# Re-ordering the opening loads, and four pair sums, of a linear-attention and token-mixer kernel

## Chip, core and metric

The kernel runs on one core of a Trainium2 chip. The metric is device microseconds of one execution. The text goes by two kinds of number: median times of several runs, and places in the trace of a single profiled run, where the start of one instruction is known to some hundredths of a microsecond. "Lead" below means how much earlier the same instruction starts in one trace than in the trace of the kernel before.

## The reference

```python
x = A_x                                        # 1 x 2048 x 1024, bf16
h = x + A(layernorm(x), wqkv, wo)              # linear attention, 32 heads
h2 = h + B(layernorm(h), w1, b1, w2, b2)       # MLP over the token axis, 3584 wide, gelu

def A(x, wqkv, wo):
    q, k, v = split(x @ wqkv)                  # heads of 32
    phi = lambda t: where(t > 0, t + 1, exp(t)) + 1e-6
    kv = einsum("bhsd,bhse->bhde", phi(k), v)
    z = einsum("bhsd->bhd", phi(k))
    o = (phi(q) @ kv) / (phi(q) @ z + 1e-6)
    return o @ wo
```

Only the very start matters here: tokens come in tiles of 128 rows. A tile is loaded, normalised (VectorE, ScalarE), transposed (TensorE), and multiplied by the key weights. Tiles 0 to 3 are done one by one with a plain product. From then on the kernel works on pairs of tiles ("runs") with a seven-product scheme, which needs sums and differences of blocks of the tokens ("pair sums") and of the weights ("weight sums").

## The kernel before: the parts concerned

The opening loads (`P` is 128, `CW` 512, `D` 1024, `ND` 8, `hk` 4). A contraction piece is 128 of the 1024 rows of the weights; "pieces 0-1" is `wkv[:, 0:2, 0:CW]`.

```python
def load_x(i, halves=False):
    x_sb = xload.tile([P, D], BF16, name="x_sb")
    if halves:
        nc.sync.dma_start(x_sb[:, 0:CW], x[i * P:(i + 1) * P, 0:CW])
        pin(nc.scalar.dma_start(x_sb[:, CW:D], x[i * P:(i + 1) * P, CW:D]))
    else:
        nc.sync.dma_start(x_sb[:], x[i * P:(i + 1) * P, :])
    return x_sb
# ...
xs = {0: load_x(0, True)}
xs[1] = load_x(1)
for k in (0, hk // 2):                                     # pieces 0-1, 2-3: ACT queue
    pin(nc.scalar.dma_start(wkv[:, k:k + hk // 2, 0:CW], wqkv_v[:, k:k + hk // 2, D:D + CW]))
nc.sync.dma_start(wkv[:, hk:ND, 0:CW], wqkv_v[:, hk:ND, D:D + CW])   # pieces 4-7
# ...
xs[2] = load_x(2)
for k0 in (0, hk):                                         # the other 512 key columns, two halves
    nc.sync.dma_start(wkv[:, k0:k0 + hk, CW:D], wqkv_v[:, k0:k0 + hk, D + CW:2 * D])
for i in range(3, G0 + 2):
    xs[i] = load_x(i)
```

The first products, in program order (every operation is pinned in its place on its engine):

```python
pin(ln[1][1](0))                 # VectorE: statistics of tile 1's first half
norm_halves(0)                   # VectorE: tile 0 normalised
transpose_first(0, 0, 0)
# ...
k_parts(0, 0, range(0, 6))       # tile 0, first key columns, pieces 0 to 5
norm_halves(1)
transpose_first(1, 6, ND)        # tile 1 transposed, pieces 6 and 7 of tile 0 between
ln_stats(2)
stats(2)                         # ScalarE: tile 2's scale
k_unit(1, 0)
# ...
k_unit(0, 1)                     # tile 0, other key columns
# ...
transpose_in(2)                  # TensorE transposes, ScalarE copies
ln_stats(3)                      # VectorE
stats(3)                         # ScalarE, behind the copies of tile 2
# ...
w_sums(kmov, slice(0, 1))
norm_halves(3)
# ...
k_unit(1, 1)
transpose_in(3)
```

And the pair sums in front of run 1, whose first use is the product `p6`:

```python
w_sums(vmov, slice(2, 4))
proj_unit(1, NDC + 1, pin)
ln_finish(G0 + 1)
x_sums(1)
# ...
v1.p1()
q_fill()
kv_accum(0)
kv_accum(1)
v1.p6()
```

## Time and profile before

| | before |
|---|---|
| time, median of the first 3 runs | 559.61 us (559.16 to 560.11) |
| profiled span | 558.6 us |
| TensorE busy | 551.3 us, 99% |
| VectorE, ScalarE busy | 444.0, 288.7 us |
| granted TensorE clock | 0.999 |

The page puts TensorE first everywhere, so the reading is about TensorE's few idle pieces; the prediction shows the view of waits and the timeline of TensorE for them. One view that the prediction did not use belongs here, because it turns out to hold the answer: the chain of work that ended last, in order of time. Its columns are start, duration, and what the chain was on; this is the kernel before.

```profile
4.08 9.13 DMA x_sb<-in_A_x_dram
...
13.23 1.30 DVE st L855 x2
...
15.36 1.22 DVE shared_sb L938
16.58 0.34 DVE xn L865
...
16.96 0.72 PE tp L1176 x8
```

The chain runs from the issue of tile 3's load straight to its landing at 13.21, through VectorE's statistics of that tile, a weight sum of 1.22 us (`w_sums(kmov, slice(0, 1))`) that stands in VectorE's order in front of the tile's normalisation, and the normalisation itself, to tile 3's transposes at 16.96. The longest wait of TensorE, the 1.56 us for weight pieces that the prediction names first, is not on it.

### The profile page before, as it was taken

How to read it: one execution, taken by the hardware profiler on the slowest of the kernel's cores; microseconds unless marked ns; L12 is line 12 of the kernel's file. 1: busy time of each engine (PE TensorE's matmuls, PEld its weight loads, DVE VectorE, ACT ScalarE, POOL GpSimd, SP SyncE). 2: the span in 40 equal slices, each digit the busy share in tenths (PEclk: the TensorE clock that was granted, in tenths of full speed). 3: DMA queues.
4: the chain of work that ended last, by engine and by line, in shares of the span. 5: the costliest groups of instructions: out<-in, count | busy, mean ns of one | idle time of the engine just before them, and what ended most of it. 6: DMA issues, size and time to landing. Idle time of an engine off the chain costs nothing.

```text
span 558.6 us, 8933 instructions
## 1 busy us (share of the span) xinstructions
PE 551.3 (99%) x3387; PEld 320.3 (57%) x3387; DVE 444.0 (79%) x858; ACT 288.7 (52%) x614; POOL 26.3 (5%) x36
## 2 busy tenths in 40 slices
PE   7999999999999999999999999999999999999997
PEld 3444446645444444456666766666444667767665
DVE  6898888764479688889989889897996978749747
ACT  4747778676777777645455565464310312413311
POOL 1000000000000000000000000000002103103111
PEclk9999999999999999999999999999999999999999
DMA  8933332201955961102240431414768759849434
GB/s 296 308 76 76 76 76 39 39 0 48 338 144 167 340 207 75 76 0 70 84 151 0 151 115 38 150 33 100 191 214 226 196 126 247 213 131 239 95 105 75
DMA packets 83931, 74.51 MB, mean 133 GB/s; under 512 B 15650, under 2 KB 76336, under 8 KB 83888
## 3 DMA queue, kind: packets, MB, share of 16 engines
q1 hardware_dynamic: 79104, 69.61, 41.7%
q0 software_dynamic: 4096, 3.68, 4.8%
q10 hardware_dynamic: 688, 0.66, 0.4%
q8 instruction: 26, 0.43, 0.3%
q14 instruction: 17, 0.14, 0.1%
HBM read 59.12 MB, written 11.67 MB: 127 GB/s over the span
## 4 chain that ended last, share of the span: by engine, by line
PE 90%; DMA 5%; DVE 3%; ACT 1%; issue 1%; SPq 0%; DVEq 0%; ACTq 0%
PE psI L234 23%; PE psC L234 14%; PE acc_t L234 14%; PE psB L234 8%; PE psB L964 4%; PE psC L964 4%; PE psA L964 4%; PE psA L346 2%; PE acc_t L1295 2%; PE psB L346 2%; DMA x_sb<-in_A_x_dram 2%; PE psE L964 2%; PE psC L346 2%; DMA wq<-in_B_w_dram 2%; PE acc_t L886 2%; PE psA L234 1%
## 5 line engine op out<-in xcount | busy, mean ns | idle before, releaser
L234 PEld LDWEIGHTS <-is 128*128 128x128 f16 x736 | 71.8, 98 | 31.2 <-DVE hi L234 0.4
L234 PEld LDWEIGHTS <-sa 128*128 128x128 f16 x606 | 59.2, 98 | 27.4 <-issue 0.2
L234 PEld LDWEIGHTS <-wq 128*128 128x128 bf16 (+1 forms) x496 | 48.4, 98 | 28.2 <-issue 1.0
L234 PE MATMUL acc_t<-wo_sb,pqT 128*128 128x512 f16 x256 | 55.6, 379 | 0.0
L491 POOL DMA_DIRECT2D out_dram<-wq x28 | 24.4, 935 | 520.6 <-ACT wq L494 489.1
L234 PEld LDWEIGHTS <-pqT 128*128 128x128 bf16 x256 | 24.9, 98 | 30.5 <-issue 0.6
L234 DVE TENSOR_TENSOR t<-psI,t 128x256 f32<-128x256 f32 (+1 forms) x45 | 20.8, 476 | 22.2 <-PE psI L234 20.9
L194 DVE TENSOR_SCALAR e_sb<-e_sb 128x512 bf16<-128x512 bf16 x64 | 18.5, 288 | 22.0 <-ACT e_sb L189 21.9
L234 PE MATMUL psC<-gs,wq 128*128 128x512 f16 x140 | 34.1, 379 | 0.0
L964 PEld LDWEIGHTS <-xs 128*128 128x128 f16 x208 | 20.0, 98 | 22.5 <-DVE xs L953 1.1
L234 PE MATMUL psC<-hT,sa 128*128 128x512 f16 x112 | 31.2, 379 | 0.0
L234 PE MATMUL psI<-hi,is 128*128 128x256 f16 x200 | 30.0, 273 | 0.0
L234 PE MATMUL psB<-hT,sa 128*128 128x512 f16 x112 | 29.7, 379 | 0.0
L234 PE MATMUL acc_t<-xnT,wq_sb 128*128 128x512 bf16 x128 | 29.5, 380 | 0.1
L189 ACT ACTIVATE e_sb<-acc_t 128x512 bf16<-128x512 f32 x32 | 19.1, 598 | 18.6 <-PE acc_t L1295 10.0
L234 DVE BATCH_NORM_STATS2 hst<-acc_t 128x6 f32<-128x512 f32 x32 | 21.4, 692 | 9.0 <-ACT h_bf L234 8.9
L964 PE MATMUL psA<-wkv,xnT 128*128 128x512 bf16 x104 | 26.7, 379 | 0.0
L964 PEld LDWEIGHTS <-xnT 128*128 128x128 bf16 x156 | 15.2, 98 | 18.1 <-issue 0.2
L234 PE MATMUL psC<-hT,wq 128*128 128x512 f16 x96 | 24.6, 379 | 0.0
L234 ACT CAST h_bf<-acc_t 128x512 bf16<-128x512 f32 x32 | 18.4, 581 | 12.0 <-PE acc_t L234 12.0
L234 DVE TENSOR_TENSOR e<-psI,es 128x256 f32<-128x256 f32 x20 | 8.5, 425 | 19.9 <-PE psI L234 17.8
L234 ACT COPY psI<-psI 128x256 f32<-128x256 f32 x50 | 18.0, 360 | 11.6 <-PE psI L234 9.7
(246 smaller groups left out, 1132.6 us busy)
## 6 DMA issues: line engine op xcount, KB each, us to landing
wq<-in_B_w_dram SPq DMA_DIRECT2D x14, 1024.0 KB, 7.9
wq<-in_B_w_dram SPq DMA_DIRECT2D x12, 896.0 KB, 8.0
gs<-parked SPq DMA_DIRECT2D x9, 896.0 KB, 4.8
shared_sb<-rd_dram SPq DMA_DIRECT2D x32, 128.0 KB, 3.8
out_dram<-h_bf SPq DMA_DIRECT2D x16, 256.0 KB, 2.0
x_sb<-in_A_x_dram SPq DMA_DIRECT2D x15, 256.0 KB, 3.0
w2o<-in_B_w_dram SPq DMA_DIRECT2D x4, 896.0 KB, 10.8
out_dram<-wq POOLq DMA_DIRECT2D x28, 128.0 KB, 5.0
```

What stands on the lines that cost most here:

```text
L189: pin(nc.scalar.activation(e_sb[:], src, ACT.Exp))
L194: pin(nc.vector.tensor_scalar(e_sb[:], e_sb[:], 1.0, PHI_EPS, ALU.min, ALU.add))
L234: return (lambda *a, **kw: pin(op(*a, **kw))) if self.always or getattr(Held, self.key) else op
L346: pe.matmul(ps[:, cols], lhsT=lhs[:, k, :], rhs=mv(k)[:, cols], start=(start and k == 0), stop=(k == self.nk - 1), skip_group_check=True,)
L491: nc.gpsimd.dma_start(to, ot[:, a:b], accum_op=ALU.add)
L886: mm = nc.tensor.matmul(pp[:, 0:CW], lhsT=xnT[:, kt, i * P:(i + 1) * P], rhs=wkv[:, kt, c * CW:(c + 1) * CW], start=(kt == 0), stop=(kt == ...
L964: pin(nc.tensor.matmul(ps[:], lhsT=lhs[:, k, :], rhs=rhs[:, k, :], start=(start and k == 0), stop=(k == hk2 - 1), skip_group_check=True,))
L1295: nc.tensor.matmul(qp[:, 0:SW], lhsT=wq_sb[:, kt, j * P:(j + 1) * P], rhs=xnT[:, kt, u * SW:(u + 1) * SW], start=(kt == 0), stop=(kt == ND ...
```

## The change

Intent: put the opening loads on SyncE in the order in which they are first wanted, so that pieces 2-3 no longer land behind pieces 4-7; let tile 1 come on the ACT queue beside them; fetch tile 3 in front of the second half of the other key columns; and make run 1's pair sums ahead of two weight sums that are wanted later.

```diff
-            def load_x(i, halves=False):
+            def load_x(i, halves=False, q=nc.sync):
 ...
-                    nc.sync.dma_start(x_sb[:], x[i * P:(i + 1) * P, :])
+                    dma = q.dma_start(x_sb[:], x[i * P:(i + 1) * P, :])
+                    if q is not nc.sync:
+                        pin(dma)
 ...
-            xs[1] = load_x(1)
-            for k in (0, hk // 2):
-                pin(nc.scalar.dma_start(wkv[:, k:k + hk // 2, 0:CW], wqkv_v[:, k:k + hk // 2, D:D + CW]))
-            nc.sync.dma_start(wkv[:, hk:ND, 0:CW], wqkv_v[:, hk:ND, D:D + CW])
+            xs[1] = load_x(1, q=nc.scalar)
+            for k0, k1 in ((0, hk // 2), (hk // 2, hk), (hk, ND)):
+                nc.sync.dma_start(wkv[:, k0:k1, 0:CW], wqkv_v[:, k0:k1, D:D + CW])
 ...
             for k0 in (0, hk):
                 nc.sync.dma_start(wkv[:, k0:k0 + hk, CW:D], wqkv_v[:, k0:k0 + hk, D + CW:2 * D])
-            for i in range(3, G0 + 2):
+                if k0 == 0:
+                    xs[3] = load_x(3)
+            for i in range(4, G0 + 2):
                 xs[i] = load_x(i)
 ...
+            x_sums(1)
             w_sums(vmov, slice(2, 4))
             proj_unit(1, NDC + 1, pin)
             ln_finish(G0 + 1)
-            x_sums(1)
```

## The prediction

> **What bounds the kernel now.** I read the page first. TensorE is busy for 551.3 of 558.6 us and leads the chain of work that ended last with 90%, at full granted clock in all 40 slices. So time can only be won where TensorE is idle, 7.3 us in all. The view of waits, filtered to TensorE and with no window, names every idle piece of it that a semaphore ended:
>
> ```profile
> PE acc_t L886 <- DMA wkv<-in_A_wqkv_dram: 1.6, 1, 1.6
> PE acc_t L98 <- DVE warm L88: 1.2, 1, 1.2
> PE tp L1176 <- DVE xn L865: 0.6, 2, 0.3
> PE psB L964 <- DVE xs L953: 0.3, 1, 0.3
> PE acc_t L234 <- ACT r_sb L191: 0.2, 1, 0.2
> ```
>
> Columns: total us, times, longest. All but the last row lie in the first 36 us. The 1.2 is the wait for the very first operand. So the whole stock that this change can reach is 1.6 + 0.6 + 0.3 = 2.5 us, 0.45% of the span. The rest of the idle time stands at the launch and behind the last matmul, and the change does not touch it.
>
> The timeline of TensorE places these pieces (start, duration, what, and in brackets the idle time before it):
>
> ```profile
> 6.08 0.72 PE L1176 MATMUL tp<-ident,xn 128*128 128x128 bf16 x8 [0.22 <-DVE xn L865]
> 6.94 0.60 PE L886 MATMUL acc_t<-wkv,xnT 128*128 128x512 bf16 x2
> 9.10 1.02 PE L886 MATMUL acc_t<-wkv,xnT 128*128 128x512 bf16 x4 [1.56 <-DMA wkv<-in_A_wqkv_dram]
> ...
> 16.96 0.72 PE L1176 MATMUL tp<-ident,xn 128*128 128x128 bf16 x8 [0.33 <-DVE xn L865]
> ...
> 35.56 1.04 PE L964 MATMUL psB<-wo_sb,xs 128*128 128x512 f16 x4 [0.28 <-DVE xs L953]
> ```
>
> The first projection runs its contraction pieces 0 and 1 at 6.94, then stands until 9.10, because pieces 2 and 3 of the key weights have not landed. At 16.96 it waits for token tile 3's normalised rows; at 35.56 for the pair sums of run 1. From 17.5 to 35.3 and after 36.4 TensorE never stands.
>
> The DMA view, windowed to single issues, gives the landings. Key-weight pieces 0-1 (ACT queue, issued 1.18) land at 5.0, tile 1 (SyncE, 1.20) at 4.4, pieces 4-7 (SyncE, 1.66) at 8.8, pieces 2-3 (ACT, 1.67) at 9.06, tile 2 (2.13) at 9.5; the two halves of the other key columns at 11.0 and 12.5, tile 3 at 13.2. The two loads that matter:
>
> ```profile
> wkv<-in_A_wqkv_dram SPq DMA_DIRECT2D x1, 512.0 KB, 7.2
> wkv<-in_A_wqkv_dram ACTq DMA_DIRECT2D x1, 256.0 KB, 7.4
> ```
>
> The last number is us to landing: a load half the size takes longer on the ACT queue. Pieces that are needed first come last.
>
> **What the Trainium skill says.** "DMA: Bandwidth & Descriptors", section "Queues, rings and completion order": each of the 16 engines takes turns between the queues that it has work for. The trace agrees: both loads above were issued within 0.01 us and end 0.2 us apart, so pieces 2-3 were held back by pieces 4-7. Same page, "Issuing engines are not separate DMA queues": another issuing engine brings no bandwidth, only issue time. So tile 1 on the ACT queue is a matter of order alone. Same page, "Specifications": about 358 GB/s from HBM for a core. The trace's stretches show 351 from 6 to 8 us, 373, 369, then 354 and 353: up to 4% above the page, and full from 6 us until 25 us. Nothing makes these loads faster; they can only be sorted. "VectorE: DVE Perf Modes", section "Side-by-side: where the cycles go for N=2048 bf16": about 1224 ns for a two-source 16-bit operation of that length; the trace has 1219 to 1226 ns for the weight sums.
>
> **The change part by part.** No arithmetic and no byte is added.
>
> *Key weights.* In order of need, 128 KB + 256 KB of tile 0's halves and pieces 0-1 come first on SyncE, beside 128 + 256 KB on ACT; then pieces 2-3 (1.05 MB in all by then), pieces 4-7 (1.57 MB), tile 2 (1.84 MB), the same sums as before for the last two. How fast these land is the uncertain size. The sixteen completion steps of each load stand in the trace. Until 5.2 us those of one load lie within 0.4 us of each other; for pieces 4-7 they spread from 6.2 to 8.84 with a middle of 7.1, so a few of the 16 engines fell behind by up to 1.8 us between 5 and 9 us. They never catch up before 24 us: the last step stays 1.4 us or more behind the middle one. Two cases follow.
>
> Case L (the lag returns): the slowest engine's landings by bytes are 0.79 MB at 5.0, 1.57 at 9.0, 1.84 at 9.5, 2.36 at 11.0. Then pieces 2-3 land at 5.0 + (1.05-0.79)/(1.57-0.79) x 4.0 = 6.3, pieces 4-7 at about 8.9. TensorE does pieces 0 to 3 from 6.94 to 7.8 (0.216 us each) and waits for piece 4 until 8.9, where it stood at 9.53 before: 0.6 us ahead. Tile 2 still lands at 9.5. The second half of the other key columns, now behind tile 3, comes at 3.15 MB, 13.2, where TensorE would want it at about 12.8: a new wait of 0.4 us, after which 0.2 us of lead are left. Tile 3 now lands at 11.8 instead of 13.2. That alone does not give 1.4: VectorE is at tile 2's normalisation until 12.4 (before, 12.82), so tile 3's statistics start 0.8 us earlier. ScalarE must copy tile 2's transposes, 0.2 us earlier, before it makes tile 3's scale; so the scale is at 16.0 instead of 16.22, the normalised rows start at 16.06 instead of 16.50, and the transposes of 16.96 start at 16.5. **Gain 0.4 us.**
>
> Case N (no lag): pieces 2-3 at 5.8, 4-7 at 7.4, tile 2 at 8.1, tile 3 at 10.3, the late key columns at 11.8. Pieces 0 to 5 run from 6.94 to 8.3, tile 1's transposes then wait for its rows (8.11, first half written 8.52), so TensorE is there at 8.55 instead of 9.96, 1.4 us ahead. The statistics of tiles 2 and 3 follow at once, and the transposes of 16.96 start at 15.5. **Gain 1.45 us.** The limit is then ScalarE and VectorE, no longer a load.
>
> *Tile 1 on ACT.* It trades places with pieces 0-1 and should land between 4.3 and 5.0. VectorE takes its first statistics at 4.93, so at worst this costs 0.1 us in front of tile 0's rows.
>
> *Pair sums earlier.* Four operations of 0.42 us, 0.35 to 0.45 from start to start, 1.47 together, move ahead of two weight sums (31.94 to 34.25). The second pair sum is then ready at about 33, where TensorE wants it at 35.28: the whole wait of **0.28 us** goes. In exchange, tile 5's normalisation goes from 34.16 to 35.6 and its transposing load lands at about 39.2 instead of 37.8. Its first reader is the pair sums of run 2 at 40.68, so 1.4 us remain. The third value-weight sum is ready at 34.6 and wanted at 39.9. VectorE's work is the same and it has 0.68 us of idle time at 39.85, so the 0.28 isn't given back.
>
> *Sum.* Case L: 0.4 + 0.28 = 0.7 us. Case N: 1.45 + 0.28 = 1.7 us. After 36 us TensorE has no wait but one of 0.2, so what is won there should reach the end one for one. I weigh L somewhat more than N, since the small bias loads and the traffic mix that lie in the same microseconds stay: 1.1 us. Before: 559.61. Predicted: **558.5 us**.
>
> **Rivals.** (1) *A wait takes the place of the one removed.* The late key columns behind tile 3, or tile 1's transposes, or tile 3's rows. Speaking for it: the load stream is full from 6 to 25 us, and landings in front of TensorE have under 1 us of slack. If it takes all, only 0.28 stays: 559.3. (2) *Tile 1 late on the ACT queue.* Its statistics stand in VectorE's fixed order ahead of tile 0's normalisation, so every 0.1 us beyond 4.93 delays the first transposes. Against it: the ACT queue's first 384 KB landed by 5.0 before. If it came at 6.0 as the ACT load of 7.4 us suggests, about 1 us would be lost at the start, though the weights would meanwhile arrive: 559.0 to 560.0. (3) *Nothing comes through,* because a later load or buffer sets the pace. Against it: TensorE has no idle time between 36 us and its end but 0.2. It would give 559.6. (4) All 2.5 us are gained, 557.1. Against it: tile 3's rows depend on ScalarE's and VectorE's chain.
>
> **Range and chances.** Case L to case N is 558.9 to 557.9; runs of the kernel before differ by 0.95 us (559.16 to 560.11), a median of three by some 0.4. I take 557.4 to 559.6. Two per cent would be 11.2 us, over four times the whole stock of 2.5 us, so faster has 1%. Slower would need a stall of 11 us that nothing here could make: 1%.
>
> **What would show it.** Right: the 1.56 us wait at 9.10 is gone or below 0.9, pieces 2-3 land before 7 us, the wait for pair sums at 35.56 is gone, TensorE starts its last transposes between 15.5 and 16.6. Wrong, if tile 0's transposes start later than 6.2 (rival 2), if the wait for the key columns of k_unit(0, 1) is over 0.5 us (rival 1), if tile 5's transposing load delays the sums of run 2, or if the lead at 36 us isn't found at the end of the span (rival 3).

## The result, and the profile after

| | before | after |
|---|---|---|
| time, median of 6 runs | 559.57 us (559.16 to 560.11) | 558.97 us (558.64 to 559.96) |
| ratio, 95% interval | 1 | 0.9992 (0.9979 to 1.0005) |
| second measurement: median, ratio | 559.60 us, 7 runs | 558.72 us, 4 runs; 0.9980 (0.9965 to 0.9995) |
| profiled span | 558.6 us | 557.7 us |

A ratio is the mean time of one kernel's runs over that of the other's in the same rounds, so it is not quite the ratio of the two medians. The second measurement excludes equality, the first does not; both point to half a microsecond or one.

First the view of TensorE's waits of the changed kernel, to be set against the five rows in the prediction (total us, times, longest):

```profile
PE acc_t L98 <- DVE warm L88: 1.2, 1, 1.2
PE acc_t L234 <- ACT r_sb L191: 0.4, 1, 0.4
PE tp L1179 <- DVE xn L867: 0.3, 1, 0.3
PE acc_t L888 <- DMA wkv<-in_A_wqkv_dram: 0.3, 1, 0.3
PE psB L234 <- ACT psB L530: 0.2, 1, 0.2
```

The 1.6 for key weights has become 0.3, and the row for pair sums is gone. In exchange a row that was 0.2 is 0.4 and a new one of 0.2 stands at the bottom; both lie far behind the opening. The timeline of TensorE in the changed kernel:

```profile
6.33 0.72 PE L1179 MATMUL tp<-ident,xn 128*128 128x128 bf16 x8 [0.33 <-DVE xn L867]
7.19 1.76 PE L888 MATMUL acc_t<-wkv,xnT 128*128 128x512 bf16 x6
...
12.72 1.02 PE L888 MATMUL acc_t<-wkv,xnT 128*128 128x512 bf16 x4 [0.26 <-DMA wkv<-in_A_wqkv_dram]
...
16.02 0.72 PE L1179 MATMUL tp<-ident,xn 128*128 128x128 bf16 x8
...
34.16 1.02 PE L966 MATMUL psB<-wo_sb,xs 128*128 128x512 f16 x4
```

Pieces 0 to 5 of tile 0 are now one row of six matmuls. The merged row hides a short wait: the fifth matmul starts 0.51 us behind the fourth (8.35 after 7.84, against a pace of 0.22), just behind the landing of pieces 4-7 at 8.31. The new wait at 12.72 is for the second half of the other key columns, which were put behind tile 3; the prediction foresaw it. Tile 3's transposes start 0.94 us earlier than before, run 1's product 1.40 us. The DMA view for single issues shows pieces 4-7 (512 KB) and pieces 2-3 (256 KB), with us to landing last:

```profile
wkv<-in_A_wqkv_dram SPq DMA_DIRECT2D x1, 512.0 KB, 6.1
wkv<-in_A_wqkv_dram SPq DMA_DIRECT2D x1, 256.0 KB, 4.3
```

The needed one comes first now. But the chain that ended last shows that the opening still hangs on a load, only on another one:

```profile
4.48 8.20 DMA wkv<-in_A_wqkv_dram
...
12.72 1.02 PE acc_t L888 x4
...
14.01 1.07 ACT xnT L1189 x2
15.08 0.20 ACT lnv L863
...
15.31 0.21 ACT rstd L864
...
15.54 0.42 DVE xn L867
...
16.02 0.72 PE tp L1179 x8
```

From the late key columns' landing at 12.68 the chain goes over the product that needs them, tile 2's transposes, ScalarE's copies of these, ScalarE's scale for tile 3, VectorE's normalisation, to tile 3's transposes.

A weight load is TensorE's instruction that takes in the fixed operand of the matmuls behind it; its rows are marked PEld. Following single weight loads through both traces (3400 in each; the same instructions in the same order) gives the lead: -0.25 us at tile 0's transposes, +1.48 at piece 2, +0.95 at tile 3's transposes, +1.45 at run 1's product, +1.25 at 156 us, +0.97 at the end. So half a microsecond of what was won at the opening was lost again later. Where and why is a question for the experiments.

### The profile page after: what moved, and what is told of

It is laid out like the page before. It is cut to its first block, busy times and chain, and to the rows that moved or that the text cites. A ratio compares the mean times of both kernels' runs of the same rounds, so it can differ in the third digit from the quotient of the medians.

```text
span 557.7 us, 8915 instructions
## 1 busy us (share of the span) xinstructions
PE 550.7 (99%) x3370; PEld 320.4 (57%) x3387; DVE 443.8 (80%) x858; ACT 288.8 (52%) x614; POOL 26.2 (5%) x36
## 4 chain that ended last, share of the span: by engine, by line
PE 91%; DMA 4%; DVE 2%; ACT 1%; SPq 1%; issue 0%; DVEq 0%; ACTq 0%
PE psI L234 23%; PE psC L234 14%; PE acc_t L234 14%; PE psB L234 8%; PE psC L966 4%; PE psB L966 4%; PE psA L966 4%; PE acc_t L888 3%; PE acc_t L1298 2%; PE psB L346 2%; PE psA L346 2%; PE psE L966 2%; PE psC L346 2%; DMA wq<-in_B_w_dram 2%; DMA wkv<-in_A_wqkv_dram 1%; PE kvps L917 1%
```

## The experiments

Twelve runs were made, of eight new kernels and four repeats, all with correct output. Two theories are compared. **Theory 1**, the prediction's: the wait for pieces 2-3 was what held TensorE, and the order of need removed it. **Theory 2**, from the chain: only the last of the loads that tile 3's transposes depend on counts, and the waits in front of it are interchangeable. Of the first four runs, the expectation of "tile 1 on SyncE" still rests on theory 1; theory 2 was written down, as the last landing plus a constant, after these four, from their traces. Then a further question came up: is the landing of that last load a matter of chance or of layout?

### Each part alone

Sums alone:

```diff
 # the kernel before, with only
+            x_sums(1)
             w_sums(vmov, slice(2, 4))
             proj_unit(1, NDC + 1, pin)
             ln_finish(G0 + 1)
-            x_sums(1)
```

> The kernel before with the pair sums moved and its loads untouched. Theory: nothing moves ahead of 31 us, so the transposes of tile 3 start at 16.96 as before (within 0.2), and run 1's product with the second pair sum starts 0.46 us earlier than before (35.1 instead of 35.56), since TensorE's weight loads stood 0.46 us there although the waits view shows 0.28. Rival: only the 0.28 us shown as idle comes back (35.28). Time: 0.3 to 0.5 us less than before, within the noise of the runs.

Measured: 559.17 us (median of 4), ratio 0.9990 (0.9974 to 1.0005). Transposes of tile 3 at 16.86, run 1's product at 34.95 (weight load) instead of 35.55: the lead grows from 0.10 to 0.60, so the pair sums are worth **0.50 us**, not 0.28. The reason is visible in the weight-load row of the kernel before:

```profile
35.55 0.55 PEld L964 LDWEIGHTS <-xs 128*128 128x128 f16 x4 [0.46 <-DVE xs L953]
```

The matmul row has 0.28 us of idle time in front of it, this one 0.46. Ends of matmuls are modelled and overlap the next ones, so the idle time in front of a matmul is too small a number for what a wait costs; start to start the trace has 0.56 against a pace of 0.06 here.

This run holds something more valuable. Its loads are those of the kernel before, yet pieces 2-3 landed at 7.10 instead of 9.06, and the waits read:

```profile
PE tp L1176 <- DVE xn L865: 1.5, 2, 1.0
PE acc_t L98 <- DVE warm L88: 1.2, 1, 1.2
PE acc_t L886 <- DMA wkv<-in_A_wqkv_dram: 0.5, 1, 0.5
```

The wait for weights fell from 1.6 to 0.5 without any change to it, and all that came of it at tile 3's transposes is 0.10 us: the wait for tile 3's rows grew to 1.0. Theory 1 is in doubt from here on.

Loads alone:

```diff
 # the changed kernel, with
-            x_sums(1)
             w_sums(vmov, slice(2, 4))
             proj_unit(1, NDC + 1, pin)
             ln_finish(G0 + 1)
+            x_sums(1)
```

> The changed kernel with the pair sums put back behind the weight sums. Theory: the loads alone give the 0.95 us lead at tile 3's last transposes (16.0 against 16.96), and the wait for the pair sums comes back, so the lead at run 1's product is 0.95 and not 1.45. Rival: with TensorE earlier the wait for the pair sums grows beyond 0.46 and the lead falls under 0.8. Time: some 0.5 to 0.9 us below before.

Measured: 559.04 us (4 runs), ratio 0.9987 (0.9971 to 1.0004). Lead 1.30 at tile 3's transposes, more than the changed kernel's 0.95 with the same loads, because the late key columns landed at 12.34 instead of 12.68. No growth up to run 1's product: the wait for pair sums is back in full (start-to-start 0.55). It did not grow with the lead either, so the rival fell. The two parts add up: the sums give 0.50 us with the old loads (0.10 to 0.60) and with the new ones (0.95 to 1.45).

### Which load counts

Tile 3 back behind both halves of the late key columns:

```diff
             for k0 in (0, hk):
                 nc.sync.dma_start(wkv[:, k0:k0 + hk, CW:D], ...)
-                if k0 == 0:
-                    xs[3] = load_x(3)
+            xs[3] = load_x(3)
```

> The changed kernel with tile 3 back behind both halves of the other key columns. Theory: the new 0.26 us wait at 12.7 is gone, but tile 3 lands 1.5 us later (12.7), its normalised rows start near 16.1 instead of 15.5 and the transposes near 16.5, so about 0.4 us of the 0.95 are lost (lead 0.4 to 0.6). Rival: tile 3's place does not matter because ScalarE's chain sets its rows; then the lead is 1.2.

Measured: 559.83 us (4 runs), ratio 1.0000 (0.9985 to 1.0015). Tile 3 landed at 12.75, the transposes started at 16.50, lead 0.46, as expected of the theory; TensorE stood 0.91 us there for tile 3's rows. With the pair sums this trace has a lead of 0.96 us at its end, of which the four timed runs show nothing: that is how little four runs can tell here.

Pieces 4-7 in front of pieces 2-3, all else as changed:

```diff
-            for k0, k1 in ((0, hk // 2), (hk // 2, hk), (hk, ND)):
+            for k0, k1 in ((0, hk // 2), (hk, ND), (hk // 2, hk)):
```

> The changed kernel with pieces 4-7 in front of pieces 2-3 on SyncE, tile 1 still on ACT: the order of need undone for the wait of 1.56 us that the prediction named first. Theory: pieces 2-3 land last of the first half, at about 8.0 to 8.4, so TensorE stands some 0.7 us there, but the lead at tile 3's transposes stays that of the changed kernel (0.95 to 1.4), since these start at the landing of the late key columns (12.1 to 12.75 with tile 1 on ACT) plus 3.33 at the earliest. Rival, the prediction's step: the order of these pieces is what gained, and the lead falls below 0.5.

Measured: 558.54 us (4 runs), ratio 0.9978 (0.9965 to 0.9991). Lead 1.37 at tile 3's transposes, at least as good as with the pieces in order of need (0.95 and 1.39 in the changed kernel's two traces over the same trace of before). The test was weaker than planned: pieces 2-3 landed at 7.79, and TensorE stood only 0.2 us there (7.41 to 7.83 from start to start, against a pace of 0.22) instead of 0.7. And the chain of this trace goes back to that very landing:

```profile
2.17 5.62 DMA wkv<-in_A_wqkv_dram
...
7.83 1.02 PE acc_t L888 x4
...
15.59 0.72 PE tp L1179 x8
```

Still, the part of the change that the prediction put first could be undone without loss in this trace. That it would be so with pieces 2-3 later than 7.79 and the last load as early as here (11.96) is not shown.

Now all fourteen traces can be laid side by side. "Last load" is whichever of tile 3 and the late key columns landed last.

| trace | tile 1 on | tile 3 | late key columns | tile 3's transposes start | minus last load |
|---|---|---|---|---|---|
| before | SyncE | 13.21 | 12.54 | 16.96 | 3.75 |
| before, second trace | SyncE | 13.38 | 12.68 | 17.14 | 3.76 |
| sums alone | SyncE | 13.10 | 12.42 | 16.86 | 3.76 |
| tile 3 last | ACT | 12.75 | 12.08 | 16.50 | 3.75 |
| after | ACT | 11.18 | 12.68 | 16.01 | 3.33 |
| after, second trace | ACT | 10.63 | 12.13 | 15.57 | 3.44 |
| loads alone | ACT | 10.84 | 12.34 | 15.66 | 3.32 |
| pieces swapped | ACT | 10.47 | 11.96 | 15.59 | 3.63 |
| store first (below) | ACT | 11.53 | 13.03 | 16.36 | 3.33 |
| store first, second trace | ACT | 10.70 | 12.19 | 15.51 | 3.32 |
| weights on ACT (below) | SyncE | 11.72 | 13.20 | 16.53 | 3.33 |
| weights on ACT, second trace | SyncE | 11.45 | 12.94 | 16.26 | 3.32 |
| all on SyncE (below) | SyncE | 11.59 | 13.08 | 16.41 | 3.33 |
| split (below) | ACT | 11.44 | 12.19 | 15.60 | 3.41 |

Where tile 3 comes last, the transposes start 3.75 us behind it, four times of four. Where the late key columns come last, they start 3.33 us behind these, seven times of ten. In the other three that would be at 15.3 to 15.5, and they start at 15.57 to 15.60, set by other chains: from tile 1's landing in two, from pieces 2-3 in the one with the pieces swapped. In the eleven, whose last landings lie between 12.19 and 13.38, no wait further in front enters, and theory 2 holds; its floor is at about 15.5. So the load part of the change is worth 3.75 - 3.33 = **0.42 us** by its order, for taking tile 3 out of the last place, plus whatever it does to the landing of the last load. That second part is the larger one: of the lead of 0.95 us in the first pair of traces, 0.53 is the earlier landing (13.21 to 12.68), and of the 1.57 in the second pair it is 1.25 (13.38 to 12.13).

The 3.75 us hold the weight sum of 1.22 us. In the second trace of before, tile 3's scale was ready at 15.71, but its normalisation started at 16.68, behind that sum (15.54 to 16.76). No run moved the sum behind the normalisation, so what this would have given, with the loads left alone, is open.

### Chance or layout

Tile 1 back on SyncE and pieces 0-1 on ACT, pieces 2-3 still in front of 4-7:

```diff
-            xs[1] = load_x(1, q=nc.scalar)
-            for k0, k1 in ((0, hk // 2), (hk // 2, hk), (hk, ND)):
+            xs[1] = load_x(1)
+            pin(nc.scalar.dma_start(wkv[:, 0:hk // 2, 0:CW], wqkv_v[:, 0:hk // 2, D:D + CW]))
+            for k0, k1 in ((hk // 2, hk), (hk, ND)):
```

> The changed kernel with tile 1 back on the SyncE queue and weight pieces 0-1 back on ACT; pieces 2-3 stay ahead of 4-7 on SyncE. Theory: tile 1 lands at about 4.4 instead of 5.24, tile 0's transposes start at 6.1 instead of 6.33, but piece 4 still lands near 8.3, so TensorE only waits longer there and the lead at 16 us stays within 0.1 of 0.95: the swap of queues is worth nothing, the order of pieces 2-3 and 4-7 is worth all. Rival: the 0.25 us at the start go through to the end (lead 1.2).

Measured: 558.60 us (4 runs), ratio 0.9983 (0.9966 to 1.0000). Tile 1 landed at 4.53 and tile 0's transposes started at 6.10 as expected. But pieces 4-7 came at 8.84 and the late key columns at 13.20, half a microsecond later than in the changed kernel, and the lead was 0.43. The expectation of 0.95 missed, and with it that the order of pieces 2-3 and 4-7 is worth all; so did the rival's 1.2. Whether the late landing was luck or came with the layout, one trace could not say, so four kernels were run on one chip.

> The kernel before once more, for a second profile. In five profiles so far the start of tile 3's transposes is the landing of the last of two loads plus a constant: tile 3 + 3.75 us where tile 3 comes last, the late key columns + 3.33 where these come last. Theory A (chance): that last landing varies by half a us from run to run whatever the layout, so it can fall anywhere from 12.3 to 13.2 here. Theory B (layout): with weight pieces on the ACT queue it is always late, so it is 13.0 to 13.3 here, and the transposes start at 16.8 to 17.0. The wait of 1.56 us for pieces 2-3 may be another (0.5 in the run with only the sums moved) and that does not matter.

> The changed kernel once more. Theory A: the last landing (late key columns, 12.68 before) may fall anywhere from 12.3 to 13.2. Theory B: with tile 1 on ACT it is 12.3 to 12.8. Both: transposes of tile 3 at that landing plus 3.33, lead at run 1's product larger than that at the transposes by 0.5.

> Tile 1 on SyncE, weight pieces 0-1 on ACT, all else as changed; second profile. Theory B: the late key columns land at 13.0 to 13.3 again (13.20 before), transposes of tile 3 at 16.3 to 16.6. Theory A: anywhere from 12.3 to 13.2.

All on SyncE (`xs[1] = load_x(1)` in the changed kernel, in front of the weights):

> The changed kernel with tile 1 on SyncE in front of all weights, so that ACT carries only the half of tile 0. Theory B: no weight load shares the engines with a weight load of another queue, so the late key columns land at 12.3 to 12.8 as in the changed kernel, and tile 1 lands a little earlier than 5.24: lead as the changed kernel. Theory A: anywhere. If the swap to ACT itself were what helps, this would land at 13.2.

Measured, last load of the group: kernel before 13.38, changed kernel 12.13, weights on ACT 12.94, all on SyncE 13.08. Times: 559.51, 558.72, 559.08 and 559.82 us (4 runs each), ratios 0.9995, 0.9980, 0.9983 and 0.9995. The waits of the second trace of the kernel before:

```profile
PE tp L1176 <- DVE xn L865: 1.5, 2, 1.0
PE acc_t L98 <- DVE warm L88: 1.2, 1, 1.2
PE acc_t L886 <- ACT lnv L861: 0.3, 1, 0.3
PE acc_t L234 <- ACT r_sb L191: 0.3, 1, 0.3
PE psB L964 <- DVE xs L953: 0.3, 1, 0.3
PE acc_t L886 <- DMA wkv<-in_A_wqkv_dram: 0.3, 1, 0.3
```

The same kernel that waited 1.6 us for key weights in its first trace waits 0.3 in its second, and its transposes of tile 3 start not earlier but 0.18 us later. That is the plainest proof that this wait cost nothing of its own in this layout.

As to layout: over all traces the last load came at 12.0 to 13.0 with tile 1 on ACT (eight traces, mean 12.41) and at 12.9 to 13.4 with tile 1 on SyncE (six traces, mean 13.15). The two sets overlap by a single trace, the store-first one at 13.03. Chance within a layout is large: two traces of one kernel differ by up to 0.84 us (store first, 13.03 and 12.19). But it is unlikely to be all: on each of the two chips that are known to have run both (15 and 6), every trace with tile 1 on ACT was earlier than every one with it on SyncE. The trace at 13.03 is from a third chip (3), where only kernels with tile 1 on ACT were traced. My own version of the layout reading, that weight loads on two queues hinder each other, fell: with no weight on ACT but tile 1 on SyncE the landing was as late as before. The version left is that tile 1 on the ACT queue itself goes with an earlier end. Why, no run tells. What the trace shows is that late landings come from a few of the sixteen completion steps of a load: in the kernel before, pieces 4-7 have their middle step at 7.1 and their last at 8.84, in the changed kernel's second trace 7.2 and 7.75. The middle step of the last load lies at 11.5 to 12.1 in all fourteen traces, its last step 0.3 to 1.7 us behind. And the spread is there before 9.1 us: in thirteen traces the last load landed 4.35 to 4.40 us behind pieces 4-7, in the one with the pieces swapped 4.17 us behind pieces 2-3. A rival stands untested: the two small loads of biases that GpSimd issues at 1.3 and 2.3 us, and which the prediction names as a possible source of the lag, were the same in all runs.

### Where the lead went later

In the changed kernel's first trace the lead fell from 1.45 us at 34 us to 0.97 at the end. Two places take it. Near 155 us ScalarE stands for a DMA, and TensorE for ScalarE. The timeline, kernel before:

```profile
154.91 0.60 ACT L234 ACTIVATE shared_sb<-den_ps 128x512 f16<-128x512 f32 x1 [1.60 <-DMA rd_dram<-shared_sb]
...
156.53 0.38 PE L234 MATMUL acc_t<-wo_sb,kvT 128*128 128x512 bf16 x1 [0.21 <-ACT r_sb L191]
```

and the changed kernel:

```profile
153.66 0.60 ACT L234 ACTIVATE shared_sb<-den_ps 128x512 f16<-128x512 f32 x1 [1.76 <-DMA rd_dram<-shared_sb]
...
155.29 0.38 PE L234 MATMUL acc_t<-wo_sb,kvT 128*128 128x512 bf16 x1 [0.37 <-ACT r_sb L191]
```

ScalarE wants to overwrite the buffer of the inverse denominators, whose store has not landed. The store was issued 1.40 us earlier but landed only 1.24 us earlier. The other place is at 513 us, where VectorE waits for a weight load of the second MLP product, here the kernel before and the changed kernel:

```profile
512.50 0.63 DVE L234 TENSOR_TENSOR is<-wq 128x896 f16<-128x896 bf16 x1 [0.17 <-DMA wq<-in_B_w_dram]
```

```profile
511.52 0.62 DVE L234 TENSOR_TENSOR is<-wq 128x896 f16<-128x896 bf16 x1 [0.49 <-DMA wq<-in_B_w_dram]
```

That load was issued 1.3 us earlier and landed 0.97 us earlier. In the second pair of traces nothing is lost: 2.06 us of lead at run 1's product, 2.25 at the end. So this loss is not a fixed price of being early; it comes with loads that take half a microsecond more or less from run to run, in front of engines that have no slack for them.

The wait at 155 us can be taken away without touching the wait itself, by moving what the store queues behind: four loads of residual rows, wanted some 25 us later.

```diff
-            for i in range(XRL + 1):
-                load_xr(i)
 ...
                 if n in spread_at:
                     den_spread(spread_at[n])
+                if n == 0:
+                    for i in range(XRL + 1):
+                        load_xr(i)
```

> The changed kernel with the four residual-row loads moved from in front of the first store of the inverse denominators to behind its spread. Nothing differs before 135 us. Theory: near 155 us TensorE's weight loads stand 0.6 to 0.8 us in all (two gaps of 0.5 to 0.75 and 0.48 us against a pace of 0.22) because ScalarE waits for this store, which lands 6 us after its issue behind the residual rows; with the store first it lands about 3 us earlier and the gaps go, so the lead over before grows by 0.6 to 0.8 us from run 1's product to 160 us. Rival: the wait moves to the spread's loads or to the residual rows and nothing is gained at 200 us.

Measured: 558.23 us (4 runs), ratio 0.9969 (0.9955 to 0.9984). The opening had bad luck (13.03, the latest with tile 1 on ACT), so the lead was 1.10 at run 1's product; across 155 us it grew to 1.69 over the kernel before, whose two gaps there are 0.59 and 0.48 us. Both are 0.22 now, the pace. The end kept 1.50. Repeated:

> The changed kernel with the store first, once more, with more timed runs. Theory: TensorE's two gaps near 155 us are at most 0.5 us above pace in all, as in the first run of it, against 0.8 in the changed kernel, so 0.3 to 0.6 us are gained there whatever the loads at the start do; ratio to before 0.996 to 0.998. Rival: the first run's ratio of 0.9969 was chance and this one is at 0.9985 or above, as the changed kernel's two measurements around it.

Measured: 557.93 us (5 runs), ratio 0.9968 (0.9954 to 0.9981). The same lines as above, in this trace:

```profile
151.44 0.60 ACT L234 ACTIVATE shared_sb<-den_ps 128x512 f16<-128x512 f32 x1
152.08 0.60 ACT L189 ACTIVATE e_sb<-acc_t 128x512 bf16<-128x512 f32 x1
...
154.04 0.59 PE L234 MATMUL acc_t<-wo_sb,kvT 128*128 128x512 bf16 x2
154.24 0.60 ACT L189 ACTIVATE e_sb<-acc_t 128x512 bf16<-128x512 f32 x1 [0.59 <-PE acc_t L234]
```

ScalarE does not wait for the store any more, and TensorE has no gap. Against the changed kernel this is worth 0.6 to 0.8 us in the trace (its gaps were 0.75 and 0.48 in one trace, 0.53 and 0.48 in the other). This is the best version by its medians; against the kernel before both of its measurements exclude equality. It was not timed in the same rounds as the changed kernel; of all runs, its mean is 558.23 us (9 runs) and the changed kernel's 558.98 us (10 runs). Beside it in its first rounds ran the kernel with the pieces swapped, at 558.54 against 558.23 us, so the gain over the changed kernel is shown by the traces and not by the times.

With the late key columns split in two besides:

```diff
-            for k0 in (0, hk):
-                nc.sync.dma_start(wkv[:, k0:k0 + hk, CW:D], wqkv_v[:, k0:k0 + hk, D + CW:2 * D])
-                if k0 == 0:
+            for k0, k1 in ((0, hk), (hk, hk + hk // 2), (hk + hk // 2, ND)):
+                nc.sync.dma_start(wkv[:, k0:k1, CW:D], wqkv_v[:, k0:k1, D + CW:2 * D])
+                if k1 == hk + hk // 2:
                     xs[3] = load_x(3)
 # and the store first, as above
```

> The changed kernel with the late key columns cut in two, tile 3 between them, and the store first as in the run beside it. Theory: the last landing is 12.1 to 12.8, but now only pieces 6-7 wait for it, wanted 0.43 us later, and tile 3 lands 0.75 us before it, so tile 3's transposes start at that landing plus 2.9 to 3.0, though not before 15.5, where the chain from tile 1 sets them; with the store the lead at 160 us is 2.2 to 2.6 us over the kernel before. Time about 2 us below before (557.5). Rival: the extra load or the moved loads cost as much elsewhere, and the time is that of the changed kernel.

Measured: 558.62 us (6 runs), ratio 0.9975 (0.9963 to 0.9986). The wait at 12.7 is gone, but the last load was early in this trace (12.19), the transposes started at 15.60, their floor, and the split had nothing to win; in the unsplit store-first kernel's second trace they start at 15.51. The lead at 160 us was 2.45 as expected, and then the load at 513 us took 9.8 us from issue to landing (8.8 to 9.3 in the two traces of the changed kernel and in the kernel before), which left 1.64 behind that wait and 1.70 at the end. The expected 557.5 us was missed by a microsecond. Nothing speaks for the split.

## Why the prediction was right, and which steps were not

The predicted 558.5 us stands against 558.97 and 558.72; the gain of 1.1 us against 0.6 and 0.9. The range and the chances held. By its steps:

- *The stock of idle time, 2.5 us, so no 2% either way.* Right.
- *Waits at the opening.* Right in the traces: pieces 2-3 at 5.96 (6.3 or 5.8 predicted), pieces 4-7 at 8.31 (8.9 or 7.4), tile 3 at 11.18 (11.8 or 10.3), a new wait of 0.26 us for the late key columns (0.4), transposes between 15.5 and 16.6: 16.01.
- *What the removed wait was worth.* The text led with the 1.56 us for pieces 2-3 and called its removal the sign of success. That wait had no worth: the second trace of before had 0.3 us of it, and its transposes of tile 3 started 0.18 us later (17.14 against 16.96). The case-by-case working below it had the right mechanism all the same, since it followed the chain to tile 3's rows; case L's 0.4 us is the 0.42 of the table. The step that failed is reading the longest wait as the one that ends last. What ended last was tile 3's own load, at 13.21, 3.75 us in front of its transposes; the chain view showed it.
- *Pieces 2-3 "were held back by pieces 4-7".* A reading of one trace that others do not bear out. With the same loads in the same order, the two ended 0.2 us apart there (9.06 and 8.84), but 0.86 apart in the second trace of before (8.12 and 8.98) and 1.63 apart with the sums alone (7.10 and 8.73). A slip without effect: of the weight sums, one took 1173 ns, outside the 1219 to 1226 that the text gives.
- *Lag or no lag as two chances of the same layout, and tile 1 on ACT "a matter of order alone".* Not borne out: the last load came at 12.41 on average with tile 1 on ACT, 13.15 with it on SyncE, with one trace of fourteen overlapping. The cause stays open, and chance is a good part of the spread.
- *Tile 1 lands between 4.3 and 5.0, costing at most 0.1 us.* It landed at 5.05 to 5.32 and the first transposes were 0.25 us late against the first trace of before. But the second trace of before has tile 1 at 5.27 and the transposes at 6.37 on SyncE too; and nothing of it reached tile 3.
- *Pair sums 0.28 us.* The mechanism was right, the term too small: 0.50, in every pair of traces, because idle time in front of a matmul understates the wait. The side effects were as foreseen: tile 5's transposing load landed at 38.3 (39.2 predicted), its reader did not wait.
- *What is won at 36 us reaches the end one for one.* Wrong in the first trace, where 0.48 of 1.45 us were lost at 155 and 513 us to loads with no slack; right in the second. The prediction had seen the wait of 0.2 at 155 us and not asked what set it: a store behind loads that were not yet wanted, worth 0.6 to 0.8 us when moved, as much as the measured gain of the whole change.

The errors cancelled in part: the pair sums gave more, the later waits took some, and the last load happened to land between the two cases (12.68; 13.2 and 11.8 predicted). So it is partly luck that the number came this close.

## What to carry to other kernels

The longest wait of the busiest engine is not the one to remove; follow the chain that ended last to the load it hangs on, and ask which load becomes the last one after the change. Compare such small effects by the start of one and the same instruction in several traces of each kernel, since a single trace can differ from the next of the same kernel by half a microsecond or more. And a short wait late in the kernel can be worth as much as a long one at its start: look at what its DMA queues behind.

## What the Trainium skill lacked or had wrong

- "DMA: Bandwidth & Descriptors", section "Issuing engines are not separate DMA queues", says that issuing from several engines saves only issue time. Here the loads' last landing was 12.41 us on average with tile 1 on ACT and 13.15 with it on SyncE, for the same bytes (eight and six traces, one overlap). The cause was not found, so this is a difference to test, not a refutation.
- The same page says nothing of how far the completion steps of one load spread when the engines are full: 8.84 us for the last against 7.1 for the middle one, with the lag then carried on by every later load up to 24 us, and up to 1.1 us of difference in the last landing between traces with tile 1 on ACT (11.96 to 13.03).
- "Trainium Kernel Development and Optimization", section "Performance Expectations", calls matmul busy time a bad metric for how close a kernel is to roofline, because matmuls are pipelined. It does not say that idle time in front of a matmul suffers likewise: 0.28 us shown, 0.46 in front of the weight load, 0.50 gained when the wait went.
